# Gates, heads and output tiles in a fused attention-and-gate kernel: when the small work is done

## The chip, the cores and the metric

The kernel runs on one core of a Trainium2 chip. The time is the device time of one execution in microseconds (us); a kernel is judged by the median of its runs. The core has a matrix engine (TensorE, PE in the profile, with its weight loads as PEld), VectorE (DVE), ScalarE (ACT), GpSimd (POOL), SyncE (SP, which issues most transfers here), each with its own queue of instructions, and 16 queues of DMA. An engine works through its instructions in the order of the program; between engines semaphores say when a result is there.

## The reference

The input `x` has S = 2048 rows of D = 576 numbers. With `xn` its layer norm:

```python
qkv = (xn @ wqkv).reshape(1, S, 3, 32, 18)      # 32 heads of 18
p = softmax(q @ k.T * 18 ** -0.5)               # per head, 2048 x 2048
s = concat_heads(p @ v) @ wo
gate = relu(xn @ W_gate); up = xn @ W_up        # 576 -> 4608
g = silu((gate * up) @ W_down)                  # 4608 -> 576
out = x + s * g
```

All of it is float32.

## The kernel before

**Precision.** A float32 operand is kept as a high and a low part that TensorE can take, and a product is made of three matmuls (high x high, high x low, low x high). So every operand is *split* first: a rounding copy on one engine and a subtraction on another or the same. Weights are split on POOL (`split_pool`, lines 97 and 98).

**Stages.** Layer norm and the projections to q, k and v come first (to about 222 us of the span); their results go to DRAM (`qd`, `kd`, `vd`). Then the main loop, and at its end the output projection.

**Units.** The main loop has 144 units k = 0 to 143. A unit is one pair of a row group g (512 rows, in the order 3, 0, 1, 2) and one of 36 blocks f of 128 hidden features. It computes gate and up for them (`pg`, 54 matmuls in 27 pairs, the two halves of a pair on the upper and lower 64 rows of the array). Row groups therefore change at k = 36, 72 and 108. At the end of each even unit k > 0, `down(k - 1)` multiplies two blocks with W_down (`py`, 48 matmuls) and DVE adds the result to the four `y` tiles of the row group (line 501). When a row group is done, its four `y` tiles wait in the list `gates`; `gate_step` does one: tanh on ACT into the single buffer `e` (line 512), scale and product on POOL (513, 514), and a transfer of the gated tile to DRAM (`gd`, 515).

**Attention inside the units.** The 16 head pairs u are spread between these matmuls. From unit 16 on a head pair takes eight units (four for each half p of the rows), and a unit does, for each of two heads, 8 score matmuls `psx` with an exponential on ACT behind each (line 604) and 8 score matmuls `pm` of head pair u + 1 with a maximum on DVE behind each (line 194). A softmax needs the row maxima before the exponentials: `max_rows` turns them and stores them as two more rows of q. Units 0 to 15 have maxima of head pair 0 alone, 3 or 4 per head; units 136 to 143, the last head pair, have exponentials alone. Behind the 43 pairs of a unit (35 in the last head pair) come its 32 `po` matmuls, probabilities times v. Every fourth unit `finish` ends half a head pair: its second part `rest_`, and `max_rows`, are *tasks*, run at the end of the next even unit ahead of `down`.

**What sets the order.** `emit_unit` gives each score step a due slot among the unit's matmul pairs (the list `due`; a step with late = 0 is spread over all slots) and writes everything in that order; each engine follows the order of the program, and `i % 12 == 8` puts `gate_step` at slots 8, 20 and 32 (of 43). PSUM has 8 banks: five shared in turn by `pm`, `psx`, `py` and `pw` (`shared`), two for `pg` (`bank`, "gen"), and one for `po`, which takes one of the two `pg` of odd units below 16.

**Output.** `finish` splits the normalised heads and stores high and low part in `od` [2, 576, 2048]. After unit 143, 16 tiles of 128 rows are computed from `od` and `wo` (`pw`, 28 matmuls each), multiplied by the gated rows from `gd` (`gt`, line 746), added to `x` (747) and stored (748). Weights are loaded on SP in pieces of 128 columns, runs of 512 bytes.

Of the kernel before, what the change touches and what calls it, by code (L numbers as in the profile page):

```python
# [19 lines left out]
def kernel(  # L20
# [11 lines left out]
    P = 128  # L32
# [51 lines left out]
    od = dram.tile([2, D, S], F32, name="od")  # L84
# [113 lines left out]


    with ExitStack() as st:  # L200
# [169 lines left out]
        for g in range(NQ):  # L370
# [47 lines left out]
    def up_weights(k):
        if k >= len(units):
            return  # L420
        f = units[k][1]
        rg = wr.tile([P, KC, P], F32, name="rg")
        load2(rg, [[(wg, f * P, P)], [(wu, f * P, P)]])
        gw = ws.tile([P, 2, KC, P], F32R, name="gw")
        split_pool(gw[:, 0], gw[:, 1], rg)
        gus[k] = gw
# [15 lines left out]
    def up(k):  # L442
# [3 lines left out]
        ps = [bank("pg0"), bank("pg1") if k % 2 == 0 or k >= N1 else psO.tile([P, 512], F32, name="po")]  # L446
# [61 lines left out]
    def gate_step():  # L508
        if gates:
# [5 lines left out]
            nc.gpsimd.dma_start(gd[t * P : (t + 1) * P, :], y)  # L515

    vas = []
    for i in range(2):
# [4 lines left out]
        vas.append(va)  # L523
    def run_tasks():
# [4 lines left out]
    def max_rows(qT, mx):  # L529

        nm = two.tile([P, 2, 8], F32, name="nm")
        nx = two.tile([P, 2, 2, 8], F32, name="nx")
        vec(
            nc.vector.tensor_reduce(
                nm, mx.rearrange("p h b j c -> p h (b j) c"), axis=AX.X, op=ALU.max, negate=True
            )
        )
        nxr = nx.bitcast(F32R)
        vec(nc.vector.tensor_copy(nxr[:, :, 0], nm))
# [239 lines left out]
```

## Time and profile before

| | us |
|---|---|
| runs | 2700.24, 2700.65, 2705.1 |
| median | 2700.65 |
| profiled execution | 2709.15 |
| its span | 2707.4 |
| granted clock of TensorE over it | 0.992 |
| odd unit 35, even unit 36 | 13.94, 20.62 |
| unit 37 | 22.06 |
| end of the last `py` to the end of the span | 88.4 |

The profile is of one execution. Its span is what the traced instructions and transfers cover, the time has 1.75 us around it. In timelines a row begins with the start and the length in us, then engine, line, operation, what is written from what, its shape, and in brackets the idle time before it and whom it waited for. A unit's length is the distance between the first `pg` of it and of the next one. Groups give the busy time, the mean ns of one, and the idle time before them. Views of waits give the sum in us, how many, and the longest.

### The profile page before, as it was taken

The numbers are of one execution on the slowest core, as the hardware profiler recorded it, in microseconds if no ns is written. First come the engines' busy times: TensorE is split into PE (matmuls) and PEld (weight loads), VectorE is DVE, ScalarE is ACT, GpSimd is POOL, SyncE is SP. The second block draws the span as 40 slices with busy tenths as digits, with TensorE's granted clock in tenths as the row PEclk, the third lists the DMA queues.
The fourth block names the chain that finished last, engine by engine and source line by source line (L and its number), as shares of the span: only waits on it lengthen the run. The fifth ranks groups of instructions, "written<-read, shape, count | busy, mean of one in ns | idle before, by whom it ended". The sixth has DMA issues, their size and how long they took to land.

```text
span 2707.4 us, 54577 instructions
## 1 busy us (share of the span) xinstructions
PE 2646.0 (98%) x21852; PEld 2049.2 (76%) x21852; DVE 1947.7 (72%) x3218; ACT 1447.7 (53%) x2608; POOL 1308.3 (48%) x1084
## 2 busy tenths in 40 slices
PE   8999999999999999999999999999999999999996
PEld 6888887777767777777767777777776777777776
DVE  5426667888868888888877888888886888886211
ACT  3321125666656666666656666666656666666540
POOL 4235664444454444444454444444455444445643
PEclk9999999999999999999999999999999999999998
DMA  9745332323342222222262222222253232222247
GB/s 248 207 157 152 83 80 60 82 65 82 93 114 72 74 71 71 72 75 72 73 152 72 76 70 73 66 76 71 76 138 90 59 81 64 75 58 63 71 145 225
DMA packets 260094, 257.58 MB, mean 95 GB/s; under 512 B 30656, under 2 KB 201408, under 8 KB 259840
## 3 DMA queue, kind: packets, MB, share of 16 engines
q1 hardware_dynamic: 245632, 216.32, 31.0%
q0 software_dynamic: 14208, 37.78, 4.5%
q8 instruction: 172, 2.82, 0.5%
q14 instruction: 82, 0.67, 0.1%
HBM read 203.93 MB, written 49.55 MB: 94 GB/s over the span
## 4 chain that ended last, share of the span: by engine, by line
PE 89%; DMA 4%; POOL 3%; ACT 1%; issue 1%; SPq 1%; DVE 1%; POOLq 0%; DVEq 0%; ACTq 0%
PE pg L64 30%; PE po L64 18%; PE py L64 17%; PE pm L64 12%; PE psx L64 9%; PE pq L64 2%; PE pv L64 1%; DMA xr<-in_A_x_dram 1%; PE pw L64 1%; PE tps L70 1%; DMA rgw<-in_A_wqkv_dram 1%; DMA gt<-gd 0%; DMA rd<-in_B_W_down_dram 0%; DMA qd<-hh 0%; DMA qT<-qd 0%
## 5 line engine op out<-in xcount | busy, mean ns | idle before, releaser
L194 DVE TENSOR_REDUCE mx<-pm 128x1 f32<-128x512 f32 x2048 | 1368.4, 690 | 299.8 <-PE pg L64 133.2
L604 ACT ACTIVATE p<-psx 128x512 f32<-128x512 f32 x2048 | 1150.3, 599 | 496.8 <-PE psx L64 409.5
L64 PE MATMUL pg<-x,gw 64*128 64x512 f32 x7560 | 1389.4, 394 | 6.0 <-ACT r L470 3.7
L64 PEld LDWEIGHTS pg<-x,gw 64*128 64x128 f32 x7560 | 1080.4, 186 | 109.3 <-ACT r L470 7.2
L64 PEld LDWEIGHTS py<-dw,hh 128*128 128x128 f32 x3456 | 461.5, 188 | 63.9 <-issue 57.0
L64 PE MATMUL py<-dw,hh 128*128 128x288 f32 x3456 | 482.5, 298 | 2.7 <-DVE y L501 1.9
L97 POOL CAST gw<-rg 128x1152 fp32r<-128x1152 f32 x144 | 164.7, 1144 | 639.7 <-PE pg L64 539.7
L64 PE MATMUL po<-p,va 128*32 128x512 f32 x4096 | 471.5, 601 | 0.0
L64 PE MATMUL psx<-qT,kB 56*128 56x512 f32 x1120 | 442.7, 395 | 0.0
L64 PE MATMUL pm<-kB,qT 54*128 54x512 f32 x1120 | 429.0, 407 | 7.6 <-ACT p L604 7.6
L98 POOL TENSOR_TENSOR gw<-rg,gw 128x1152 fp32r<-128x1152 f32 x144 | 382.4, 2656 | 11.6
L64 PE MATMUL psx<-qT,kA 56*128 56x512 f32 x928 | 367.3, 396 | 0.0
L501 DVE TENSOR_TENSOR y<-py,y 128x288 f32<-128x288 f32 x544 | 233.2, 451 | 180.3 <-PE py L64 176.3
L64 PE MATMUL pm<-kA,qT 54*128 54x512 f32 x928 | 358.2, 409 | 4.8 <-ACT p L604 4.8
L64 PEld LDWEIGHTS po<-p,va 128*32 128x32 f32 x4096 | 120.7, 110 | 267.7 <-issue 259.9
L97 POOL CAST dw<-rd 128x576 fp32r<-128x576 f32 x144 | 95.9, 666 | 395.3 <-PE py L64 170.2
L64 PEld LDWEIGHTS pm<-kB,qT 54*128 54x128 f32 x1120 | 206.8, 185 | 63.8 <-issue 21.6
L64 PEld LDWEIGHTS psx<-qT,kB 56*128 56x128 f32 x1120 | 207.9, 186 | 12.8
L64 PEld LDWEIGHTS pm<-kA,qT 54*128 54x128 f32 x928 | 171.5, 186 | 54.6 <-issue 17.6
L98 POOL TENSOR_TENSOR dw<-rd,dw 128x576 fp32r<-128x576 f32 x144 | 206.0, 1430 | 11.7
L475 POOL TENSOR_TENSOR hh<-h,hh 128x512 fp32r<-128x512 f32 x144 | 185.5, 1288 | 9.1 <-ACT hh L474 9.1
L64 PEld LDWEIGHTS psx<-qT,kA 56*128 56x128 f32 x928 | 172.2, 186 | 12.2 <-ACT p L604 0.5
(86 smaller groups left out, 1602.6 us busy)
## 6 DMA issues: line engine op xcount, KB each, us to landing
rg<-in_B_W_gate_dram SPq DMA_DIRECT2D x144, 288.0 KB
rg<-in_B_W_up_dram SPq DMA_DIRECT2D x144, 288.0 KB
rd<-in_B_W_down_dram SPq DMA_DIRECT2D x144, 288.0 KB
x<-xTd SPq DMA_DIRECT2D x54, 256.0 KB
qT<-qd SPq DMA_DIRECT2D x192, 72.0 KB
od<-ol POOLq DMA_DIRECT2D x128, 72.0 KB, 2.6
qd<-hh POOLq DMA_DIRECT2D x16, 512.0 KB, 3.9
kd<-hh POOLq DMA_DIRECT2D x16, 512.0 KB, 5.0
```

What stands on the lines that cost most here:

```text
L64: return tc.keep_in_program_order(nc.tensor.matmul(*args, **kw))
L70: return tc.keep_in_program_order(nc.tensor.transpose(*args))
L97: nc.gpsimd.tensor_copy(hi, raw)
L98: nc.gpsimd.tensor_tensor(lo, raw, hi.bitcast(F32), ALU.subtract)
L194: vec(nc.vector.tensor_reduce(mx[:, h, b, j, c : c + 1], ps, axis=AX.X, op=ALU.max))
L475: nc.gpsimd.tensor_tensor(hh[:, 1], h, hh[:, 0].bitcast(F32), ALU.subtract)
L501: vec(nc.vector.tensor_tensor(ys[j][:, cs], ps, ys[j][:, cs], ALU.add))
L604: nc.scalar.activation(pts[kt][:, 2 * h + b, :], ps, AF.Exp, scale=SCALE)
```

## The change

- **Gates**: one `gate_step` in each unit (slot 8), not three; six `y` buffers, not five; the four gated tiles of the last row group stay in SBUF (`kept`) and are not sent to `gd`.
- **Heads**: stored as they are, in `od` [576, 2048], by four transfers on SP at the start of the next unit (`later`, `store`); the split comes after they are loaded again (`heads`, a copy on ACT and a subtraction on DVE).
- **Row maxima**: the 16 numbers of a row are turned once, unsplit; the split is made on POOL on the turned tile, and the 8 transfers follow, at the start of the next unit.
- **Banks**: in odd units below 16 `pg` takes the `po` bank and a shared one (`pg2`).
- **Exponentials**: `late` is -4, which makes their due slots denser and leaves the last four free.
- **Output**: tiles 0 to 3 are computed between units 142 and 143; the others in the order 4 to 7, 12 to 15, 8 to 11, with heads loaded per tile, two tiles ahead (`fetch`); `x` is added in one POOL operation per tile. The weights of `wo` lie in the former place of `kB` and of one q tile, in one tile `kq`, and in `w4`. `up_weights(0)` and `(1)` are written earlier.

```diff
-    od = dram.tile([2, D, S], F32, name="od")
+    od = dram.tile([D, S], F32, name="od")
...
                 kA = at.tile([P, NQ, 512], F32R, name="kA")
-                kB = at.tile([P, NRING - NQ, 512], F32R, name="kB")
-                for kT in (kA, kB):
-                    nc.gpsimd.memset(kT.bitcast(F32), 1.0)
-                ring[:] = [kA[:, 0], *(kB[:, i] for i in range(NRING - NQ)), *(kA[:, i] for i in range(1, NQ))]
-                qTs[:] = [at.tile([P, 2, 2, 512], F32R, name=f"qT{i}") for i in range(2)]
+                kq = at.tile([P, NRING, 512], F32R, name="kq")
+                nc.gpsimd.memset(kA.bitcast(F32), 1.0)
+                nc.gpsimd.memset(kq[:, : NRING - NQ].bitcast(F32), 1.0)
+                ring[:] = [kA[:, 0], *(kq[:, i] for i in range(NRING - NQ)), *(kA[:, i] for i in range(1, NQ))]
+                qTs[:] = [
+                    kq[:, NRING - NQ :].rearrange("p (a b) s -> p a b s", a=2),
+                    at.tile([P, 2, 2, 512], F32R, name="qT"),
+                ]
...
-    yp = pool(mid, "yp", 5, "right")
+    yp = pool(mid, "yp", 6, "right")
...
-        ps = [bank("pg0"), bank("pg1") if k % 2 == 0 or k >= N1 else psO.tile([P, 512], F32, name="po")]
+        if k % 2 and k < N1:
+            ps = [psO.tile([P, 512], F32, name="po"), shared("pg2")]
+        else:
+            ps = [bank("pg0"), bank("pg1")]
...
-    def gate_step():
+    def gate_step(spill_=True):
         if gates:
             y, t = gates.pop(0)
             e = wl.tile([P, D], F32, name="e", bufs=1)
             tc.keep_in_program_order(nc.scalar.activation(e, y, AF.Tanh, scale=0.5))
             nc.gpsimd.tensor_scalar(e, e, 0.5, 0.5, op0=ALU.mult, op1=ALU.add)
             nc.gpsimd.tensor_tensor(y, y, e, ALU.mult)
-            nc.gpsimd.dma_start(gd[t * P : (t + 1) * P, :], y)
+            if spill_:
+                nc.gpsimd.dma_start(gd[t * P : (t + 1) * P, :], y)
...
+    nms = []
+    for i in range(2):
+        nms.append(two.tile([P, 2, 16], F32, name=f"nm{i}", bufs=1))
+        nc.gpsimd.memset(nms[i], 0.0)
+    later = []
+
+    def run_later():
+        while later:
+            later.pop(0)()
+
     def run_tasks():
         while tasks:
             fn, args = tasks.pop(0)
...
 
     def max_rows(qT, mx):
 
-        nm = two.tile([P, 2, 8], F32, name="nm")
-        nx = two.tile([P, 2, 2, 8], F32, name="nx")
+        nm = nms[0]
+        nms.reverse()
         vec(
             nc.vector.tensor_reduce(
-                nm, mx.rearrange("p h b j c -> p h (b j) c"), axis=AX.X, op=ALU.max, negate=True
+                nm[:, 0].rearrange("p (h m) -> p h m", h=2), mx.rearrange("p h b j c -> p h (b j) c"),
+                axis=AX.X, op=ALU.max, negate=True,
             )
         )
-        nxr = nx.bitcast(F32R)
-        vec(nc.vector.tensor_copy(nxr[:, :, 0], nm))
-        vec(nc.vector.tensor_tensor(nxr[:, :, 1], nm, nx[:, :, 0], ALU.subtract))
         nt_ = two.tile([P, 32], F32, name="nt")
-        vec(nc.vector.transpose(nt_, nx.rearrange("p h a m -> p (h a m)")))
-        for h in range(2):
-            r = h * R + KA
-            dst = qT[r : r + 2].bitcast(F32).rearrange("a b (j q t) -> a (b j) q t", q=4, t=32)
-            for q in range(4):
-                nc.sync.dma_start(
-                    dst[:, :, q], nt_[q * 32 + h * 16 : q * 32 + h * 16 + 16, :]
-                )
+        vec(nc.vector.transpose(nt_, nm.rearrange("p a m -> p (a m)")))
+
+        def rows_():
+            nr = two.tile([P, 2, 32], F32R, name="nr")
+            split_pool(nr[:, 0], nr[:, 1], nt_)
+            for a in range(2):
+                dst = qT[KA + a :: R].bitcast(F32).rearrange("h b (j q t) -> h (b j) q t", q=4, t=32)
+                for q in range(4):
+                    nc.sync.dma_start(dst[:, :, q], nr[q * 32 : q * 32 + 16, a, :].bitcast(F32))
+
+        later.append(rows_)
 
     def block32(name):
         return two.tile([P, 512], F32, tag="ot", name=name)
+
+    def store(on, u, p):
+        for s_ in range(4):
+            h, b = divmod(s_, 2)
+            f0 = (2 * u + h) * DH
+            g = 2 * p + b
+            nc.sync.dma_start(od[f0 : f0 + DH, g * 512 : (g + 1) * 512], on[s_ * 32 : s_ * 32 + DH])
 
     def finish(po, u, p):
         ot = block32("ot")
...
             )
             on = block32("on")
             vec(nc.vector.transpose(on, tq))
-            ol = two.tile([P, 2, 512], F32R, name="ol", bufs=1)
-            nc.scalar.activation(ol[:, 0], on, AF.Copy)
-            nc.gpsimd.tensor_tensor(ol[:, 1], on, ol[:, 0].bitcast(F32), ALU.subtract)
-            for s_ in range(4):
-                h, b = divmod(s_, 2)
-                f0 = (2 * u + h) * DH
-                g = 2 * p + b
-                nc.gpsimd.dma_start(
-                    od[:, f0 : f0 + DH, g * 512 : (g + 1) * 512].rearrange("i p s -> p i s"),
-                    ol[s_ * 32 : s_ * 32 + DH].bitcast(F32),
-                )
+            later.append(lambda: store(on, u, p))
...
+        run_later()
...
-            for cnt, gen, off, late in ((nm, mx, 0.0, LATE), (ns, ex, 0.25, 0)):
+            for cnt, gen, off, late in ((nm, mx, 0.0, LATE), (ns, ex, 0.25, -4)):
...
-            if i % 12 == 8:
+            if i == 8:
...
+    kept = {}
+
+    def heads(k, hf, raw5, o5):
+
+        ks = slice(k * P, (k + 1) * P)
+        raw = block32("ro").rearrange("p (c s) -> p c s", s=P)
+        nc.sync.dma_start(raw, od[:C4, ks].rearrange("(c p) s -> p c s", p=P))
+        for i in range(2):
+            nc.sync.dma_start(raw5[i * DT : (i + 1) * DT], od[C4:D, ks])
+        nc.scalar.activation(hf[:, 0], raw, AF.Copy)
+        nc.vector.tensor_tensor(hf[:, 1], raw, hf[:, 0].bitcast(F32), ALU.subtract)
+        nc.scalar.activation(o5, raw5, AF.Copy)
+        nc.vector.tensor_tensor(o5[DT:P], raw5[DT:P], o5[DT:P].bitcast(F32), ALU.subtract)
+
+    def project(k, hf, o5, gt, xt, last=False):
+
+        for m in range(2):
+            cs = slice(m * HC, (m + 1) * HC)
+            ps = shared("pw")[:, :HC]
+            prs = []
+            for c in range(4):
+                w = wos[c]
+                prs += [(hf[:, 0, c], w[:, 0, cs]), (hf[:, 0, c], w[:, 1, cs]), (hf[:, 1, c], w[:, 0, cs])]
+            prs += [(o5, wos[4][:, i, cs]) for i in range(2)]
+            for i, (l, w) in enumerate(prs):
+                mm(ps, l, w, start=(i == 0), stop=(i == len(prs) - 1))
+            vec(nc.vector.tensor_tensor(gt[:, cs], ps, gt[:, cs], ALU.mult))
+            if last:
+                nc.vector.tensor_tensor(gt[:, cs], gt[:, cs], xt[:, cs], ALU.add)
+        if not last:
+            nc.gpsimd.tensor_tensor(gt, gt, xt, ALU.add)
+        nc.sync.dma_start(out2[k * P : (k + 1) * P, :], gt)
+
+    def rows_of(k, gt, xt):
+        if k not in kept:
+            nc.sync.dma_start(gt, gd[k * P : (k + 1) * P, :])
+        nc.sync.dma_start(xt, x2[k * P : (k + 1) * P, :])
...
+        if not more:
+            spare = [xtile(xA).rearrange("p i (c s) -> p i c s", s=P) for _ in range(2)]
+            sy = [yp.tile([P, D], F32, name="y") for _ in range(2)]
+            sx = vas[0].rearrange("p t d -> p (t d)")[:, :D]
+            sr = two.tile([P, NT, HW], F32, tag="raw", bufs=1, name="r5").rearrange("p t d -> p (t d)")
+            s5 = [two.tile([P, P], F32R, name=f"o5{i}", bufs=1) for i in range(2)]
...
+            if not more and i == PER - 2:
+                for j in range(4):
+                    heads(j, spare[j % 2], sr[:, j % 4 * P : (j % 4 + 1) * P], s5[j % 2])
+                    rows_of(j, sy[j % 2], sx)
+                    project(j, spare[j % 2], s5[j % 2], sy[j % 2], sx)
...
+    run_tasks()
+    run_later()
     down(len(units) - 1)
...
+    for y, t in gates:
+        kept[t] = y
+    order = [*range(4, 8), *range(12, 16), *range(8, 12)]
+    ready8 = {}
+
+    def fetch(n):
+        k = order[n]
+        hf = xtile(xA).rearrange("p i (c s) -> p i c s", s=P)
+        gt = kept[k] if k in kept else (ws if n % 2 else wr).tile(
+            [P, 2, KC, P] if n % 2 else [P, KC, P], F32, tag="gw" if n % 2 else "rg", name="gt"
+        )
+        if k not in kept:
+            gt = gt.rearrange("p a c s -> p (a c s)") if n % 2 else gt.rearrange("p c s -> p (c s)")
+            gt = gt[:, :D]
         xt = pp.tile([P, 4, 512], F32, tag="p", name="xr").rearrange("p a s -> p (a s)")[:, :D]
-        nc.sync.dma_start(xt, x2[k * P : (k + 1) * P, :])
-        return gt, xt
-
-    heads(order[0])
+        rows_of(k, gt, xt)
+        heads(k, hf, sr[:, k % 4 * P : (k % 4 + 1) * P], s5[k % 2])
+        ready8[n] = hf, s5[k % 2], gt, xt
...
+    fetch(0)
+    fetch(1)
     while gates:
-        gate_step()
+        gate_step(False)
+    for n, k in enumerate(order):
+        project(k, *ready8.pop(n), last=n == len(order) - 1)
+        if n + 2 < len(order):
+            fetch(n + 2)
```

ACT at the first change of row group, from the end of unit 36 to unit 38; `p<-psx` are exponentials, `e<-y` is the tanh of a gate. Before:

```order
L604 ACTIVATE p<-psx 128x512 x3
L512 ACTIVATE e<-y 128x576
L604 ACTIVATE p<-psx 128x512 x5
L512 ACTIVATE e<-y 128x576
L604 ACTIVATE p<-psx 128x512 x4
L512 ACTIVATE e<-y 128x576
L604 ACTIVATE p<-psx 128x512 x3
L470 ACTIVATE r<-pg_9967 128x512
```

and after the change:

```order
L623 ACTIVATE p<-psx 128x512 x4
L522 ACTIVATE e<-y 128x576
L623 ACTIVATE p<-psx 128x512 x12
L480 ACTIVATE r<-pg_9948 128x512
L484 ACTIVATE hh<-h 128x512
L623 ACTIVATE p<-psx 128x512 x4
L522 ACTIVATE e<-y 128x576
L623 ACTIVATE p<-psx 128x512 x12
```

The second and third tanh have moved out of unit 37, one unit further each, and all 16 exponentials of a unit stand ahead of the reading of its `pg` (`r`).

DVE at the end of an even unit with tasks, between `h` of the unit and the additions of `py`. Before:

```order
L472 TENSOR_TENSOR h<-pg_5877,r 128x512
L534 TENSOR_REDUCE nm<-mx 128x16
L539 CAST nx<-nm 128x2x8
L540 TENSOR_TENSOR nx<-nm,nx 128x2x8
L542 STREAM_TRANSPOSE nt<-nx 128x32
L560 STREAM_TRANSPOSE tq<-ot 128x512
```

and after the change:

```order
L482 TENSOR_TENSOR h<-pg_5878,r 128x512
L555 TENSOR_REDUCE nm_2958<-mx 128x16
L561 STREAM_TRANSPOSE nt<-nm_2958 128x32
L589 STREAM_TRANSPOSE tq<-ot 128x512
L592 RECIPROCAL rc<-tq 128x16
```

The cast and the subtraction are gone from this place; the rest stands as it stood.

ACT at units 140 and 141 after the change (before, no split of heads stands there):

```order
L623 ACTIVATE p<-psx 128x512 x16
L480 ACTIVATE r<-pg_33934 128x512
L484 ACTIVATE hh<-h 128x512
L705 ACTIVATE x<-ro 128x512
L707 ACTIVATE o_33180<-r_33179 128x128
L623 ACTIVATE p<-psx 128x512
L705 ACTIVATE x<-ro 128x512
L707 ACTIVATE o_33181<-r_33179 128x128
L623 ACTIVATE p<-psx 128x512 x15
```

The splits of the heads for tiles 0 and 1 (`x<-ro` for features 0 to 511, `o<-r` for the other 64) stand ahead of the first exponential of unit 141 and between it and the other 15.

More of the change, by code (lines that the diff above doesn't have):

```diff
@@ L197, in max_steps, with up_weights @@
                     yield
+    units = [(g, f) for g in (NQ - 1, *range(NQ - 1)) for f in range(NF)]
+    gus, dws, hhs = {}, {}, {}
+    N1 = NU
+    def up_weights(k):
+        if k >= len(units) or k in gus:
+            return
+        f = units[k][1]
+        rg = wr.tile([P, KC, P], F32, name="rg")
+        load2(rg, [[(wg, f * P, P)], [(wu, f * P, P)]])
+        gw = ws.tile([P, 2, KC, P], F32R, name="gw")
+        split_pool(gw[:, 0], gw[:, 1], rg)
+        gus[k] = gw
     with ExitStack() as st:
@@ L408 @@
     pp = pool(mid, "pp", 4, "right")
-    w3 = pool(mid, "w3", 1, "right")
+    w4 = pool(mid, "w4", 1, "right")
     wl = pool(mid, "wl", 2, "right")
-    yp = pool(mid, "yp", 5, "right")
-    units = [(g, f) for g in (NQ - 1, *range(NQ - 1)) for f in range(NF)]
-    gus, dws, hhs = {}, {}, {}
-    N1 = NU
+    yp = pool(mid, "yp", 6, "right")
     xcur = {NQ - 1: xs[NQ - 1]}
[L418 to L426, printed above, removed]
     def down_weights(k):
@@ L666, in out_weights @@
             nc.sync.dma_start(rd, wo[c * P : (c + 1) * P, :])
-            if c < 2:
-                w = kB.rearrange("p c s -> p (c s)")[:, c * 2 * D : (c + 1) * 2 * D]
-            elif c == 2:
-                w = qTs[0].rearrange("p a b s -> p (a b s)")[:, : 2 * D]
-            else:
-                w = w3.tile([P, 2 * D], F32R, name="wo3")
+            w = kq.rearrange("p c s -> p (c s)")[:, c * 2 * D : (c + 1) * 2 * D]
         else:
@@ L675, in out_weights @@
                 nc.sync.dma_start(rd[d * DT : (d + 1) * DT, :], wo[C4:D, :])
-            w = wr.tile([P, KC, P], F32R, tag="rg", name="wo4").rearrange("p c s -> p (c s)")
+            w = w4.tile([P, 2 * D], F32R, name="wo4")
         w = w.rearrange("p (i d) -> p i d", i=2)
@@ L689 @@
         k += 1
+    early4 = []
     for u in range(NU):
@@ L696 @@
                 out_weights(i)
-            if not more and i == PER - 1:
+            if not more and i == 4:
                 out_weights(4)
             emit_unit(k, ex, 64 // PER, mx, 64 // PER if more else 0)
+            if not more and i == PER - 2:
[3 more added lines that the diff above has]
+                    project(j, spare[j % 2], s5[j % 2], sy[j % 2], sx)
             k += 1
@@ L702 @@
             assert next(gen, None) is None
+    run_tasks()
+    run_later()
     down(len(units) - 1)
-    run_tasks()
-    order = (0, 1, 3, 2)
-    hfs, o5s = {}, {}
-    def heads(g):
-        gs = slice(g * 512, (g + 1) * 512)
-        hfs[g] = []
-        for c in range(4):
-            hf = xtile(xA)
-            nc.sync.dma_start(hf.bitcast(F32), od[:, c * P : (c + 1) * P, gs].rearrange("i p s -> p i s"))
-            hfs[g].append(hf)
-        o5s[g] = hp.tile([P, 512], F32R, tag="h", name="o5")
-        for i in range(2):
-            nc.sync.dma_start(o5s[g][i * DT : (i + 1) * DT].bitcast(F32), od[i, C4:D, gs])
```

28 lines of the change are left out of this document (3 added, 25 removed).

## The prediction

> **What bounds the kernel now.** I read the page first, then the span in stretches, one unit of the main loop each, then the waits and the timeline where a stretch was too long.
>
> ```profile
> PE 2646.0 (98%) x21852; PEld 2049.2 (76%) x21852; DVE 1947.7 (72%) x3218; ACT 1447.7 (53%) x2608; POOL 1308.3 (48%) x1084
> PE 89%; DMA 4%; POOL 3%; ACT 1%; issue 1%; SPq 1%; DVE 1%; POOLq 0%; DVEq 0%; ACTq 0%
> ```
>
> TensorE is busy 98% of the span and is 89% of the chain that ended last. The change leaves the number of its matmuls as it is, so it can win only the time in which PE waits or runs slowly, and that must be looked for stretch by stretch. Columns after the stretch: length, then busy time of PE, PEld, DVE, ACT and POOL, the granted clock, DMA share and GB/s.
>
> ```profile
> 726.76:740.70 13.94, 13.94 (x121) 9.73 (x120) 11.70 (x18) 10.18 (x18) 7.65 (x6) 1.00 0.80 190
> 740.70:761.32 20.62, 20.62 (x171) 15.88 (x167) 18.94 (x32) 11.42 (x20) 8.26 (x8) 1.00 0.75 168
> 761.32:783.38 22.06, 17.69 (x119) 10.14 (x118) 11.66 (x18) 11.35 (x21) 18.77 (x19) 0.85 0.53 143
> 783.38:804.08 20.70, 20.70 (x171) 16.43 (x167) 11.33 (x17) 13.41 (x26) 8.23 (x8) 1.00 0.32 83
> 1391.13:1412.54 21.41, 16.58 (x120) 10.02 (x120) 11.65 (x18) 11.35 (x21) 17.66 (x19) 0.84 0.55 148
> 2020.26:2039.72 19.46, 16.22 (x121) 9.56 (x120) 11.66 (x18) 11.30 (x21) 17.33 (x18) 0.91 0.47 134
> 2619.00:2699.30 80.30, 64.33 (x449) 63.03 (x447) 16.91 (x39) 3.25 (x5) 37.61 (x47) 0.94 0.77 236
> ```
>
> An ordinary odd unit (35) takes 13.94 us and an even one (36) 20.62, both with PE full. The odd units 37, 73 and 109, the first odd ones after a change of row group, take 22.06, 21.41 and 19.46. The output projection at the end has 64.33 us of PE in 80.30.
>
> **Gates.** In those three units three tanh stand among the 16 exponentials of the unit. From 400 to 2500 us (units 17 to 136) the list of PE's waits has one line, and the timeline of unit 37 shows one of its three times:
>
> ```profile
> PE pm L64 <- ACT p L604: 12.4, 3, 4.8
> 774.53 0.68 ACT L512 ACTIVATE e<-y 128x576 f32<-128x576 f32 x1 [4.41 <-POOL y L514]
> 772.35 0.66 POOL L513 TENSOR_SCALAR e<-e 128x576 f32<-128x576 f32 x1
> 773.10 1.40 POOL L514 TENSOR_TENSOR y<-y,e 128x576 f32<-128x576 f32 x1
> 737.12 3.64 PE L64 MATMUL po<-p,va 128*32 128x512 f32 x32
> 777.32 6.13 PE L64 MATMUL po<-p,va 128*32 128x512 f32 x32
> ```
>
> The third tanh wants the one buffer `e`, which POOL still multiplies for the second gate, behind a weight split. ACT idles 4.41 us with exponentials queued behind it, the score banks fill, PE waits, and afterwards the 32 attend matmuls take 6.13 us and not 3.64, at the granted clock of 0.85 above. Against 13.94 the three units lose 8.12 + 7.47 + 5.52 = 21.1 us. With one tanh per unit, `e` has a whole unit (13.9 us or more) to be freed, where POOL needs some 2.1 us (0.7 scale, 1.4 product), so the wait goes. What stays is the tanh's own time on ACT. Unit 38 has one tanh and no end-of-half tasks and takes 20.70; unit 36 has tasks and takes 20.62, of which the tasks are 0.16 (next part): one tanh costs about 0.24. Twelve of them now, three before: 9 more, 2.2 us. As the exponentials stand closer now (below), I allow 2.6. Net gain **18.5**; bounds 12 (tanh at its full 0.68 twelve times) and 21.
>
> Next late: `y`. The first block of the new group takes four `y` tiles at the end of unit 38, two of them free (six buffers); the other two need the spills of gates 0 and 1, issued in units 37 and 38, well over 10 us earlier. I cost that at nothing. Cover gone, ACT's copies of `py` would hold PE a few us at three places (rival 3).
>
> **Row maxima.** The cast and the subtraction on 16 numbers per row go from DVE; POOL does a small split, behind the weight split, and SP sends the same 8 small transfers a unit later. The rows are read four units or more later for one half and two for the other, so that is hidden.
>
> ```profile
> L539 DVE CAST nx<-nm 128x16 fp32r<-128x16 f32 x32 | 49.1, 1536 | 1.1
> L540 DVE TENSOR_TENSOR nx<-nm,nx 128x16 fp32r<-128x16 f32 x32 | 38.7, 1208 | 1.1
> 478.49 6.71 PE py L64 x48
> 513.10 6.55 PE py L64 x48
> 298.77 2.66 PE L64 MATMUL py<-dw,hh 128*128 128x288 f32 x18 [1.65 <-DVE y L501]
> PE pg L64 <- ACT r L470: 3.7, 8, 0.5
> ```
>
> DVE works at these (2.7 us a time) while `py` banks wait for its additions: a `py` block with tasks takes 6.71, one without 6.55. 31 of the 32 are such, 31 x 0.16 = **5.0** (bounds 0 and 5). The other is unit 6, where PE waits 1.65. The last row is the first phase: even units wait for both "gen" banks until ACT has read the odd unit's, 3.7 in all. Odd units now use two other banks. Together **5.4** (bounds 3 and 7, for what else the 0.5-us waits cost). `pg2` takes a shared bank from the maxima there, with 3 or 4 maxima per unit and half: nothing.
>
> **Heads unsplit.** ACT loses a copy, POOL a subtraction and four issues; SP gains four stores in front of its weight loads.
>
> ```profile
> L578 POOL DMA_DIRECT2D od<-ol x128 | 76.1, 597 | 10.5 <-POOL ol L573 9.3 <-issue 1.1
> 2690.43 0.46 SPq L724 DMA_DIRECT2D xr<-in_A_x_dram  x1
> ```
>
> POOL gives up 4 x 0.60 us of issues per half, but is 48% busy and stands on the path only at the gates, counted already. SP's later loads shift by 4 x 0.46 = 1.8 us every fourth unit, and are due a unit later. Nothing, on both sides; if a weight came 1.8 us late each time, 32 x 1.8 would be rival 1's size, but no such wait is listed now.
>
> **Exponentials due four slots earlier.** The odd unit's 13.94 less 3.64 of attends leave some 10.1 us for 43 pairs of matmuls, 0.234 a slot. Sixteen exponentials over 42 slots are one per 0.615 us, over 38 one per 0.557.
>
> ```profile
> 2570.70 8.11 ACT L604 ACTIVATE p<-psx 128x512 f32<-128x512 f32 x16 [5.14 <-PE psx L64]
> L604 ACT ACTIVATE p<-psx 128x512 f32<-128x512 f32 x2048 | 1150.3, 599 | 496.8 <-PE psx L64 409.5
> L194 DVE TENSOR_REDUCE mx<-pm 128x1 f32<-128x512 f32 x2048 | 1368.4, 690 | 299.8 <-PE pg L64 133.2 <-PE pm L64 96.1 <-PE psx L64 30.7
> ```
>
> ACT can do one per (8.11 - 0.60) / 15 = 0.50, so it still keeps up, with half the margin. The maxima share the five banks and DVE needs up to 0.69 for one, with one due per 0.72 when they are the denser kind. In the program's order a bank is asked for again 12 to 17 matmuls after its last writer, as before, on average 0.7 fewer. Between nothing and 0.3 us a unit (the margin of 0.06 lost for five banks) in some 120 units lies 0 to 36 us; since PE waits nowhere in these units now, I take 0.025 a unit, **-3**.
>
> **Tail.** Four of 16 tiles of the output projection go between units 142 and 143, the rest is fed tile by tile, split on ACT and DVE.
>
> ```profile
> 2612.36 6.64 PE L64 MATMUL py<-dw,hh 128*128 128x288 f32 x48
> 2612.53 0.60 ACT L556 ACTIVATE ot<-po 128x512 f32<-128x512 f32 x1 [1.26 <-PE po L64]
> 2619.42 0.70 DVE L560 STREAM_TRANSPOSE tq<-ot 128x512 f32<-128x512 f32 x1
> 2620.93 0.71 DVE L570 STREAM_TRANSPOSE on<-tq 128x512 f32<-128x512 f32 x1
> 2644.60 0.96 PE L64 MATMUL pw<-kB,x 128*128 128x288 f32 x6
> 2646.46 0.96 PE L64 MATMUL pw<-kB,x 128*128 128x288 f32 x6
> 2652.85 1.80 PE L64 MATMUL pw<-kB,x 128*128 128x288 f32 x6 [4.38 <-DVE gt L746]
> 2656.34 0.96 PE L64 MATMUL pw<-kB,x 128*128 128x288 f32 x6
> 2697.86 0.43 PE L64 MATMUL pw<-wo,o 128*128 128x288 f32 x2
> PE pw L64 <- DVE gt L746: 11.7, 3, 5.9
> PE pw L64 <- DMA o<-od: 3.2, 1, 3.2
> DVE gt L746 <- DMA gt<-gd: 54.1, 12, 14.2
> q1 hardware_dynamic: 10099, 20.08, 67.9%
> q1 hardware_dynamic: 9227, 7.39, 28.6%
> ```
>
> Half a tile is 2646.46 - 2644.60 = 1.86 us of PE, a tile 3.73, sixteen 59.7. From the end of `py` (2619.0) to the span's end (2707.4) are 88.4 now, of which PE waits 14.9, for `gt` above all, and loses about 5 more to the clock after waits; 9.1 lie behind the last matmul (2698.3). After: four tiles cost 14.9 before unit 143. Behind `py` PE then waits for the first heads. Their split on ACT stands in its order behind three tanh, and each tanh behind POOL's work for the one before (0.68 + 0.66 + 1.40 and gaps, 2.9 apart). The tasks now come before the additions of `py` on DVE: `ot` at 2613.1, 2.2 us of chain (2619.42 to 2621.64), first `y` done at about 2616.3, tanh at 2616.4, 2619.3 and 2622.2, the split from 2622.9 to 2623.6: a wait of **4.6** behind 2619.0. The heads themselves, stored from 2615.4 on, have till 2622.9 to come back. After a wait of that length PE is slow: the half tile behind the wait of 4.38 took 2656.34 - 2652.85 = 3.49, 1.6 more than 1.86. So 4.6 + 1.6, 12 x 3.73 = 44.8, further stalls of 2 (estimate, one of today's short ones), and 9.1: 62.1. Gain 88.4 - 14.9 - 62.1 = **11.4**. Stalls are fewer than today because `gt` is loaded ahead for four tiles and kept in SBUF for four. Bounds: heads at once and no stall, 19; today's waits of 14.9 and the 5 of slow clock again, 0.
>
> The trace has two prices for transfers: in the last 95 us 20.08 MB took 67.9% of 16 queues, 19.5 KB per us and queue; from 1000 to 1100 us, with mostly weights in runs of 512 bytes, 7.39 MB took 28.6%, 16.1. In the new tail's 4.6 + 44.8 + 3.6 = 53.0 us some ten tiles of heads in 512-byte runs (3.3 MB, 12.7 us on 16 queues) and 24 pieces of 288 KB (7.1 MB, 22.7 us) must move: 35.4 of 53.0 us or 67%, where today's share is 0.77. The Trainium skill, "DMA: Bandwidth & Descriptors", Rules for kernel authors, says to coalesce and that a transfer under 64 KB is mostly overhead, which speaks against the two 32-KB loads of heads per tile; its section on the anatomy of a DMA gives some 2 us fixed for each. By that the last 12 tiles' 24 small loads would add up to 48 us, an estimate, if each stood alone; no row here shows such loads one after another, and the sum does without it.
>
> **Against it:** the splits for the first two moved tiles stand in ACT's order ahead of, and just behind the first of, the exponentials of unit 141, and wait for heads stored at the end of unit 140 and loaded back. In that unit ACT is full (16 exponentials in one row of 8.11 us without a gap), so what it waits, PE waits soon after. The nearest row is today's wait for heads stored just before, 3.2; I take **-3**, bounds 0 and 5 (that wait and 1.6 of slow clock). Later the moved tiles' own chain (two `y`, one row buffer) lets their last two products wait some us, but unit 143 needs one bank at once: nothing, at most 5.
>
> **Sum:** 18.5 + 5.0 + 5.4 - 3 + 11.4 - 3 = 34.3. The profiled execution took 2709.15 (span 2707.4 and 1.75 around it), 8.5 above the median of 2700.65. Most terms are waits of fixed length, so I subtract from each: 2675 by the profile, **2666** by the median.
>
> **Rivals.**
> 1. Exponentials starve the banks. One mechanism: ACT's margin of 0.06 per exponential and DVE's of 0.03 per maximum do not carry the copies between them, and PE waits in every unit with scores. From 0.31 us in each of 120 units, 37 us with the 3 counted, the gain is gone; at 0.5 the time is 2666 + 57 = 2723. For it: the margin is halved. Against it: no PE wait in 2100 us but the three. Chance 0.07, the only way to slower that I see.
> 2. The tail runs at the transfers' pace: small runs twice as dear (25 us), with queues 77% busy, (25 + 23) / 0.77 = 62 us, 9 over the 53.0: 2675. For it: DVE waits 54.1 us on `gt` today at that share. Against it: today's waits are for buffers, too. Chance 0.17. (Of the Trainium skill's rules, the one above on small transfers would work this way.)
> 3. The gate change does not do what it says: a tanh is still late in each group, or the new `y` wait; from half of the 18.5 to all of it stays away: 2675 to 2685. Chance 0.08.
> 4. The moved tiles hold units 141 and 143 for 10 us in all, 7 more than counted: 2673. Chance 0.08.
>
> **How the numbers follow.** The forecast's case, 2654 to 2675 (half of each term's distance to its bounds), has 0.54; a larger gain (most terms at their better bound: 21 + 5 + 7 + 19 = 52, 2649) 0.07. Rivals 2 to 4 end at 2685 or below. The range 2649 to 2687 leaves out rival 1 and a little at both ends. About 0.2%, 5.4 us, is what a measurement of this kernel tells from no change: faster 0.91 (all but rival 1 and part of what is left), within 0.03, slower 0.06.
>
> **What would show it.** Right: units 37, 73, 109 near 14.2 us with the granted clock at 1.00 and no row of PE waiting for ACT there; every `py` block at 6.55; no wait on `r` before 400 us; some 62 us from the last `py` to the end. Wrong: rows of PE `pm` or `psx` waiting for ACT or DVE over the whole span (rival 1); PE `pw` waiting for DVE or ACT behind loads of heads (2); a PE wait over 5 us in unit 141 or 143 (4).

## The result, and the profile after

| | before | changed |
|---|---|---|
| median, us | 2702.88 | 2657.2 |
| lowest to highest, us | 2700.24 to 2710.15 | 2653.63 to 2657.88 |
| profiled execution, us (span) | 2709.15 (2707.4) | 2657.01 (2655.2) |

The ratio of the times is 0.9824, with a 95% interval of 0.9802 to 0.9847: 45.7 us faster by the medians, where 2666 was forecast, against the median of 2700.65 then known a gain of 34.3. The time lies in the range that was given, and the gain is larger than the sum. The profiled execution of before lay 6 us above its median, so the two profiles are 52.1 us apart.

The page of the changed kernel, its first line on busy time and the chain that ended last:

```profile
PE 2623.1 (99%) x21852; PEld 2023.3 (76%) x21852; DVE 1910.0 (72%) x3186; ACT 1399.6 (53%) x2608; POOL 1208.4 (46%) x971
PE 95%; DMA 2%; POOL 1%; DVE 1%; issue 0%; ACT 0%; SPq 0%; POOLq 0%; DVEq 0%; ACTq 0%
```

The number of matmuls is the same; PE's share of the chain has risen from 89% to 95%. The same stretches as before, of the changed kernel: units 35, 36, 37, 73 and 109, and the tail (columns as in the prediction):

```profile
721.93:735.76 13.83, 13.83 (x121) 9.63 (x120) 11.74 (x18) 9.85 (x18) 7.53 (x6) 1.00 0.75 174
735.76:756.19 20.43, 20.43 (x170) 15.88 (x167) 17.01 (x30) 10.44 (x19) 7.40 (x8) 1.00 0.82 183
756.19:770.25 14.06, 14.06 (x119) 9.57 (x119) 11.53 (x18) 10.17 (x19) 10.16 (x9) 1.00 0.65 168
1373.53:1387.60 14.07, 14.07 (x120) 9.26 (x119) 11.53 (x18) 10.17 (x19) 10.10 (x9) 1.00 0.63 162
1990.62:2004.70 14.08, 14.08 (x120) 9.29 (x120) 11.53 (x18) 10.17 (x19) 10.08 (x9) 1.00 0.39 110
2604.00:2651.00 47.00, 46.94 (x336) 46.45 (x334) 26.58 (x47) 9.93 (x22) 20.00 (x14) 0.95 0.68 210
```

The three units after a change of row group have lost their excess and have a clock of 1.00. An ordinary odd unit is 13.83 and not 13.94, an even one 20.43 and not 20.62, which nothing in the sum foresaw for the odd ones. All the waits of PE in the changed kernel:

```profile
PE tps L70 <- ACT xn L280: 12.7, 3, 11.3
PE pw L64 <- ACT x L705: 4.3, 1, 4.3
PE tps L70 <- ACT xn L283: 4.1, 1, 4.1
PE psx L64 <- DVE y L722: 2.2, 1, 2.2
PE pg L64 <- POOL gw L98: 2.0, 1, 2.0
PE pg L64 <- POOL gw L97: 1.3, 1, 1.3
PE psx L64 <- ACT p L623: 0.3, 1, 0.3
PE psx L64 <- DVE h L482: 0.2, 1, 0.2
```

The lines on `pm` behind exponentials (12.4), on `r` (3.7), on `py` and on `gt` (11.7) are gone. What is new is short: `pw` behind a split of heads on ACT, and `psx` of unit 143 behind the moved tiles.

Stretch by stretch, after minus before in the two profiles (unit starts read from the first `pg`): start to unit 0, 226.47 - 222.12 = +4.4; units 0 to 15, 165.5 - 172.2 = -6.7; units 16 to 135, 2058.6 - 2094.4 = -35.8; units 136 to 140, -1.9; from unit 141 to the end, 125.4 - 137.5 = -12.1. The sum is -52.1. The first of them is not counted as a gain or loss of the change: up to there the programs differ in little more than where things lie in memory and the weights of units 0 and 1, which the changed kernel asks for earlier, and unit 0 starts between 219.8 and 226.7 in the seven profiles with the old start and between 219.9 and 227.7 in the five with the new one.

### The profile page after: what moved, and what is told of

The parts are those of the page before. It is cut to its first block, busy times and chain, and to the rows that moved or that the text cites. A ratio compares the mean times of both kernels' runs of the same rounds, so it can differ in the third digit from the quotient of the medians.

```text
span 2655.2 us, 54665 instructions
## 1 busy us (share of the span) xinstructions
PE 2623.1 (99%) x21852; PEld 2023.3 (76%) x21852; DVE 1910.0 (72%) x3186; ACT 1399.6 (53%) x2608; POOL 1208.4 (46%) x971
## 4 chain that ended last, share of the span: by engine, by line
PE 95%; DMA 2%; POOL 1%; DVE 1%; issue 0%; ACT 0%; SPq 0%; POOLq 0%; DVEq 0%; ACTq 0%
PE pg L64 31%; PE po L64 18%; PE py L64 17%; PE pm L64 11%; PE psx L64 9%; PE pq L64 4%; PE pv L64 2%; PE pw L64 2%; PE tps L70 1%; DMA rd<-in_B_W_down_dram 0%; POOL dw L98 0%; DMA rgw<-in_A_wqkv_dram 0%; POOL gw L98 0%; DMA kd<-hh 0%; DMA rg<-in_B_W_up_dram 0%
## 5 line engine op out<-in xcount | busy, mean ns | idle before, releaser
L623 ACT ACTIVATE p<-psx 128x512 f32<-128x512 f32 x2048 | 1096.6, 603 | 583.9 <-PE psx L64 538.3
L64 PEld LDWEIGHTS pg<-x,gw 64*128 64x128 f32 x7560 | 1023.6, 187 | 108.1 <-issue 3.0
L98 POOL TENSOR_TENSOR gw<-rg,gw 128x1152 fp32r<-128x1152 f32 x144 | 382.6, 2657 | 11.7
L64 PE MATMUL psx<-qT,kq 56*128 56x512 f32 x608 | 231.1, 394 | 0.0
L64 PE MATMUL pm<-kq,qT 54*128 54x512 f32 x608 | 228.8, 399 | 0.1
L484 ACT ACTIVATE hh<-h 128x512 fp32r<-128x512 f32 x144 | 90.9, 631 | 220.5 <-DVE h L482 220.5
L64 PE MATMUL psx<-kq,kA 56*128 56x512 f32 x512 | 196.7, 395 | 0.3 <-DVE h L482 0.2
L64 PE MATMUL psx<-kq 56*128 56x512 f32 x512 | 195.5, 394 | 0.0
L64 PE MATMUL pm<-kq 54*128 54x512 f32 x512 | 194.6, 402 | 0.0
L64 PE MATMUL pm<-kA,kq 54*128 54x512 f32 x512 | 194.1, 400 | 0.0
L64 PE MATMUL psx<-qT,kA 56*128 56x512 f32 x416 | 160.1, 398 | 2.6 <-DVE y L722 2.2
```

The source lines that it names most:

```text
L64: return tc.keep_in_program_order(nc.tensor.matmul(*args, **kw))
L98: nc.gpsimd.tensor_tensor(lo, raw, hi.bitcast(F32), ALU.subtract)
L484: nc.scalar.activation(hh[:, 0], h, AF.Copy)
L623: nc.scalar.activation(pts[kt][:, 2 * h + b, :], ps, AF.Exp, scale=SCALE)
```

## The experiments

**Exponentials alone.** The kernel before with one number changed.

```diff
-            for cnt, gen, off, late in ((nm, mx, 0.0, LATE), (ns, ex, 0.25, 0)):
+            for cnt, gen, off, late in ((nm, mx, 0.0, LATE), (ns, ex, 0.25, -4)):
```

> The kernel before with the exponentials due four slots earlier, and nothing else. Profile of the changed kernel: an ordinary odd unit 13.84 us where before had 13.94, an even one 20.40 where before had 20.52 without tasks. Theory A (the packing does it, by a cheaper order of the matmuls): units 13.84 and 20.42, with tasks 20.58; some 120 units x 0.1 = 12 us faster, the group-change units still 19 to 22. Theory B (my prediction's sign: packing costs 0.025 a unit, and the 0.1 comes from another part): units 13.94 or a little more, the whole 0 to 4 us slower.

2691.73 us against 2700.93 (ratio 0.996, 0.9946 to 0.9974). Units 35, 36 (with tasks) and 37 of this kernel, its only long wait of PE in the main loop, and the end of the pairs of unit 45; the last fence has the same place in unit 45 of the kernel before:

```profile
725.95:739.81 13.86, 13.86 (x120) 9.99 (x120) 11.75 (x18) 9.86 (x18) 7.51 (x6) 1.00 0.80 195
739.81:760.49 20.68, 20.68 (x172) 15.94 (x168) 19.03 (x32) 11.08 (x20) 8.41 (x8) 1.00 0.70 167
760.49:779.39 18.90, 16.20 (x121) 9.35 (x120) 11.80 (x18) 11.07 (x21) 16.84 (x18) 0.91 0.54 165
PE pm L64 <- ACT p L604: 10.3, 3, 4.7
913.12 0.40 PE L64 MATMUL pm<-kB,qT 54*128 54x512 f32 x2
913.46 3.64 PE L64 MATMUL po<-p,va 128*32 128x512 f32 x32
```

```profile
917.68 0.52 PE L64 MATMUL pm<-kB,qT 54*128 54x512 f32 x2
918.13 1.07 PE L64 MATMUL po<-p,va 128*32 128x512 f32 x8
```

Theory A for the units' lengths: an odd unit takes 13.83 on average and an even one without tasks 20.43 (before 13.94 and 20.53), 0.1 less each, and the sign in the prediction's sum was wrong. An even unit with tasks stays at 20.68, so alone this is worth 0.1 in some 87 units, about 9 us, and not the 12 of all 120 (by the medians the whole kernel gains 9.2). The rest of the 13 us between the two profiles' units 16 to 135 is the three group-change units, 58.5 in all for 62.9. The place shows too: from the last two `pm` to the attends 913.46 - 913.12 = 0.34, where before had 0.45. With four free slots no score step of the exponentials stands among the last, and the two `pm` there get their banks sooner; that this is why is argued, not shown. With the row maxima moved as well, the units with tasks gain the 0.1 too: 20.49 in the rows-alone kernel, 20.39 in the kernel with four parts below.

**Gates alone.** The kernel before, five `y` buffers, without a third tanh in odd units.

```diff
-            if i % 12 == 8:
+            if i == 8 or (k % 2 and i == 32):
```

> The kernel before with at most two gates in an odd unit (slots 8 and 32) and one in an even one, so that no third tanh stands in units 37, 73 and 109; five y buffers stay. Theory A (the single e buffer and the third tanh make the stall): units 37, 73, 109 at 14.4 us or less with the granted clock at 1.00, no PE wait for exponentials, 18 to 20 us faster in the profile. Theory B (it is POOL's load or the y spills at the group change, and not the third tanh): a wait stays in units 37 to 39, less than 8 us won.

2687.6 us (ratio 0.9946, 0.993 to 0.9963). Unit 37, and the one line of PE's waits from 400 to 2500 us:

```profile
762.53:776.64 14.11, 14.11 (x121) 9.53 (x120) 11.73 (x18) 10.75 (x20) 12.77 (x15) 1.00 0.72 199
PE py L64 <- DVE y L501: 0.3, 1, 0.3
```

Theory A, to the size in the profiles: units 37, 73 and 109 take 14.10 to 14.11 and units 16 to 135 2074.2 for 2094.4. By the medians it is 13.3 us (2687.6 for 2700.93). Three tanh in one unit made the stall. The edit also puts 24 slots and not 12 between the two that stay, and lowers POOL's load in that unit (12.77 us for 18.77), so it doesn't tell these apart; for the single buffer `e` speaks the third tanh of unit 37 before, which waited 4.41 us for POOL's product of the second.

**Row maxima alone.** The kernel before with `max_rows`, `nms`, `later` and `run_later` of the changed one.

```diff
-        vec(nc.vector.tensor_copy(nxr[:, :, 0], nm))
-        vec(nc.vector.tensor_tensor(nxr[:, :, 1], nm, nx[:, :, 0], ALU.subtract))
...
+            split_pool(nr[:, 0], nr[:, 1], nt_)
...
+        later.append(rows_)
```

> The kernel before with the row maxima turned once, split on POOL and stored a unit later, and nothing else. Theory A (the cast and the subtraction on DVE hold up the additions of py): every py block with tasks 6.55 instead of 6.71, unit 6 at 14.4 instead of 16.3; 5.0 + 1.9 = 7 us faster. Theory B (the rest of the tasks on DVE is enough to hold py up): py stays at 6.65 or more, 2 us or less.

2690.77 us (ratio 0.9957, 0.9942 to 0.9972). A `py` block with tasks, unit 6, unit 37, and PE's wait for exponentials:

```profile
475.10 6.56 PE py L64 x48
283.67:298.00 14.33, 13.84 (x111) 12.19 (x108) 9.47 (x18) 2.46 (x4) 10.82 (x10) 1.00 0.28 82
757.18:775.40 18.22, 16.09 (x119) 9.70 (x118) 11.82 (x18) 11.18 (x21) 15.25 (x15) 0.91 0.53 160
PE pm L64 <- ACT p L615: 6.7, 3, 2.4
```

Theory A holds: `py` with tasks is 6.56 as without, unit 6 went from 16.30 to 14.33. That is 31 x 0.16 + 2 = 7. The other 3 are a second effect that neither theory had: the group-change units are 18.2 to 18.5 here, with waits of 6.7 and not 12.4. The three units take 55.0 in all here, 62.9 in the kernel before, 58.5 and 58.7 in the exponentials-alone and the banks-alone kernel, which leave the gates as they were: the stall is not the same in each execution, and how much of the difference is chance stays open. The profiled execution of before has the largest of them, and lay above its median: what is read from it for the gates is at the upper end.

**Banks alone.** The kernel before with the two banks for odd units below 16.

```diff
-        ps = [bank("pg0"), bank("pg1") if k % 2 == 0 or k >= N1 else psO.tile([P, 512], F32, name="po")]
+        if k % 2 and k < N1:
+            ps = [psO.tile([P, 512], F32, name="po"), shared("pg2")]
+        else:
+            ps = [bank("pg0"), bank("pg1")]
```

> The kernel before with the two other banks for pg in odd units below 16, and nothing else. Theory A (the 0.5-us waits on r are all there is): the even units of the first phase 14.56 and 14.38 become 13.9 to 14.1, 3.7 us faster. Theory B (the waits cost more than their length, by what stands behind them): 13.8 and 13.6 as in the changed kernel, some 5 to 6 us. Theory C (the shared bank pg2 delays the maxima): no gain.

2698.64 us (ratio 0.9992, 0.9981 to 1.0002): not told apart from before by the times. The profile tells more; units 4 and 6, and two waits of PE before 400 us:

```profile
263.54:277.37 13.83, 13.83 (x113) 12.42 (x110) 10.26 (x18) 2.46 (x4) 10.57 (x8) 1.00 0.33 87
284.36:299.84 15.48, 13.82 (x110) 12.51 (x107) 12.53 (x20) 2.47 (x4) 10.54 (x8) 1.00 0.29 78
PE pg L64 <- POOL gw L97: 3.5, 1, 3.5
PE pg L64 <- POOL gw L98: 1.5, 1, 1.5
```

Units 4 to 14 take 0.8 less each (14.62 to 13.83, 16.30 to 15.48), theory B; six of them are 4.8 us. But unit 1, which gains too, only waits longer for its weights: POOL's split ends when it ends, and unit 2 starts at 237.8 as before. Of a gain ahead of a wait for something else nothing arrives.

**Four parts, old tail.** The kernel before with these four (gates as in the gates-alone kernel).

> The kernel before with four parts together: exponentials due earlier, no third tanh in an odd unit, the row maxima on POOL a unit later, two other banks for pg below unit 16. Heads and output projection as before. Theory A (the parts add, each at its own place, and the rest of the gain is the tail's): unit 16 to 136 as in the changed kernel, 2058 to 2060 us where before had 2094; the end from unit 143 on 104 to 107 us as before; the whole 9 to 12 us slower than the changed kernel, 33 to 37 us faster than before. Theory B (heads stored unsplit take load from POOL and ACT and carry part of the gain inside the units): 2064 us or more between units 16 and 136.

2662.74 us (ratio 0.9846, 0.9828 to 0.9865). Units 16 to 135 take 2057.7, where the changed kernel has 2058.6: theory A. The parts inside the loop add up, by the times too (the four ratios multiply to 0.9856), and the unsplit heads carry nothing there. The tail is the old one:

```profile
PE pw L64 <- DVE gt L761: 8.7, 3, 6.4
PE pw L64 <- DMA o<-od: 4.8, 1, 4.8
```

From unit 141 to the end it takes 136.6, the changed kernel 125.4. So the new tail is worth 11.2 us by the profiles. By the medians it is 5.5 (2662.74 and 2657.2), less than the 9 to 12 expected, and the intervals of the two ratios overlap: the tail's gain is read from one execution each.

**The tail, three ways.** All three are the changed kernel with edits. The first computes no tiles between units 142 and 143:

```diff
-            if not more and i == PER - 2:
-                for j in range(4):
...
-    order = [*range(4, 8), *range(12, 16), *range(8, 12)]
+    order = [*range(0, 8), *range(12, 16), *range(8, 12)]
```

> The changed kernel with all 16 tiles of the output projection at the end, in the order 0 to 7, 12 to 15, 8 to 11, none between units 142 and 143. Theory A (moving only shifts matmul time and costs the two waits it makes): unit 141 at 11.9 instead of 13.0, unit 143's pairs at 8.4 instead of 12.9, 14.9 us more behind them, no new stalls: 5 us faster than the changed kernel. Theory B (the tail is paced by transfers, and 16 tiles in a row run into it): PE waits of more than 5 us behind loads of heads or of gated rows, no faster or slower.

the second moves the last gates behind the first tiles:

```diff
-    while gates:
-        gate_step(False)
     for n, k in enumerate(order):
...
         if n + 2 < len(order):
             fetch(n + 2)
+        gate_step(False)
```

> The changed kernel with the last four gates issued one each after the first four projected tiles, and not ahead of them. Theory A (the first pw waits for its split behind three tanh on ACT): the wait of 4.34 us falls to 1 to 2 us, the clock stays, 4 to 6 us faster. Theory B (the load of the heads stored just before sets that wait): the wait stays above 3.5 us, 0 to 1 us faster.

and the third does both.

> Both of the two: all 16 tiles at the end, and the last gates after the first tiles. Theory A (the waits are separate): 10 us faster than the changed kernel, PE from the end of the last py to the last matmul 59.7 us of matmuls and 1 to 2 of wait. Theory B (gates and loads then collide later in the tail): the gain of one is lost again, PE waits in the middle of the tail.

| from | changed | no tiles moved | gates later | both |
|---|---|---|---|---|
| median, us | 2657.2 | 2655.5 | 2652.98 | 2654.46 |
| unit 141 | 12.97 | 12.00 | 13.74 | 11.98 |
| unit 142 and moved tiles | 33.34 | 18.49 | 33.35 | 18.49 |
| unit 143 to the end of the span | 79.06 | 96.87 | 77.57 | 92.18 |
| sum | 125.4 | 127.4 | 124.7 | 122.7 |

The ratios to before are 0.9826 (0.9803 to 0.985), 0.9818 (0.9799 to 0.9837) and 0.9812 (0.979 to 0.9834): by the times none is told apart from the changed kernel. The profiles order them, one execution each. Waits of PE ahead of `pw`, without moved tiles, then with later gates:

```profile
PE pw L64 <- ACT x L705: 7.7, 4, 4.3
PE pw L64 <- DVE x L706: 0.8, 4, 0.2
PE pw L64 <- DVE o L708: 0.7, 1, 0.7
```

```profile
PE pw L64 <- DVE o L708: 1.6, 1, 1.6
PE pw L64 <- ACT x L705: 1.3, 1, 1.3
```

Without moved tiles the two waits that moving makes are gone, 5.4 us, but theory A fails: new waits of 4.9 us (9.2 listed, less the 4.3 ahead of the first tile) and slow clock behind them stand in the middle of the tail, and the sum is 2 worse. With later gates the wait ahead of the first tile falls from 4.3 to 1.3, theory A for the cause; but the clock behind it still falls to 0.50 for 3.4 us (2604.44 to 2607.85), a new wait of 1.6 takes half of the gain, and unit 141, which the edit doesn't touch, is 0.8 longer in this profile (`psx` waits 0.74 for an addition of `py`): 0.7 is left. Both together are 2.7 better, where theory A said 10.

**A tail with more room.** No moved tiles, heads loaded into the `xr` buffers (four and not two), one gate after every third tile.

```diff
-        raw = block32("ro").rearrange("p (c s) -> p c s", s=P)
+        raw = raw.rearrange("p (c s) -> p c s", s=P)
...
+        xt, raw = xp[:, :D], xp[:, D : D + 512]
...
+        if n % 3 == 1:
+            gate_step(False)
```

> The changed kernel with all 16 tiles at the end, heads loaded beside the rows of x (four buffers and not two), and the last four gates after the tiles 2, 5, 8 and 11 of the tail. Theory A (in the two kernels without moved tiles PE waits in the middle of the tail because two head buffers and the tanh in ACT's order hold the splits back): PE waits in the tail fall from 7 to 9 us to 3 or less, from unit 143 to the end 87 to 89 us, 6 to 8 us faster than the changed kernel. Theory B (the transfers themselves are the pace): the waits stay at 6 us or more, from unit 143 on 92 us or more.

2653.97 us (ratio 0.9813, 0.9795 to 0.9832), from unit 143 on 92.2: theory B by its number, but neither theory by the waits of PE, 4.2 ahead of `pw`. PE's waits from unit 143 on, ACT's for loaded heads and the whole tail of this kernel, then ACT's waits in the changed kernel's tail:

```profile
PE pw L64 <- ACT x L705: 2.8, 2, 1.4
PE pw L64 <- DVE x L706: 1.4, 4, 0.9
PE py L64 <- DVE y L511: 1.7, 1, 1.7
ACT x L705 <- DMA xr<-od: 41.4, 12, 5.1
2571.00:2639.00 68.00, 63.62 (x452) 61.54 (x450) 30.86 (x64) 13.84 (x31) 30.28 (x23) 0.97 0.68 206
```

```profile
ACT x L705 <- DMA ro<-od: 19.3, 8, 4.2
ACT o L707 <- DMA r<-od: 6.5, 2, 5.0
```

With buffers to spare ACT still waits for heads to land, but little of it reaches PE: from the last `py` to the last matmul it takes 67.4 us for 59.7 of matmuls, 4.2 of the rest in waits and some 1.7 (an estimate) at a clock of 0.50 that lasts 3.4 us; the other 1.8 are not listed anywhere. The 1.7 ahead of that is another matter: a split of heads on DVE stands between the additions of `py`. The transfers' pace is not shown: queues are at 0.68 over this tail as in the changed kernel's 47 us, which has 5 us at 0.97 (2615 to 2620) without a wait. The two tiles of heads that PE waited for, 1.4 us each, were asked for late: SP issues their loads at 2606.98 and 2611.97, behind the store of a finished tile, and their splits begin 4.2 and 5.1 us later. How much of that is the order on SP and how much the transfers stays open. So does the worth of moving four tiles: in the profiles it gains 2.0 with the gates first (125.4 for 127.4) and loses 2.0 with the gates late (124.7 for 122.7).

**The end of the span.** In the kernel before, 9.1 us lie between the last matmul and the end, in the changed one 4.3. The trace shows POOL's closing drain until 2706.58, 9.2 us behind POOL's last addition (2697.34); in the changed kernel 3.3 (2649.23 to 2652.51), within the landing of the last output. The kernel before with the transfers of gated tiles and heads issued by SP:

```diff
-            nc.gpsimd.dma_start(gd[t * P : (t + 1) * P, :], y)
+            nc.sync.dma_start(gd[t * P : (t + 1) * P, :], y)
...
-                nc.gpsimd.dma_start(
+                nc.sync.dma_start(
                     od[:, f0 : f0 + DH, g * 512 : (g + 1) * 512].rearrange("i p s -> p i s"),
```

> The kernel before with the transfers of gated tiles and of heads issued by SP and not by POOL, to see what the end of the span hangs on: before, 9.1 us lie between the last matmul and the end, with POOL's closing drain 9.2 us behind its last addition; the changed kernel has 4.3. Theory A (POOL's late software transfers lengthen its drain): 4 to 5 us behind the last matmul. Theory B (something else, such as POOL's many additions): 7.7 us or more as in all four kernels with the old tail.

2688.34 us, one run. The drain ends 2.3 us behind POOL's last addition (2680.47 to 2682.77). The span ends 6.0 us behind the last matmul, between the two theories, but 3.0 behind DVE's last addition (2683.53, late by a row of `x`), as in the changed kernel (3.3), and not 8.1 as before: theory A for the drain, on this single execution. Unit 37, and PE's waits for exponentials in the whole run:

```profile
758.50:776.22 17.72, 16.19 (x120) 9.62 (x119) 11.71 (x18) 11.19 (x21) 14.56 (x13) 0.90 0.64 177
PE pm L64 <- ACT p L604: 4.6, 3, 1.9
```

The three group-change units take 51.5 in all, less than in any other kernel that keeps the gates (55.0 to 62.9). POOL's issues no longer stand between its products there; that this is why is argued, since the stall differs between executions.

## Why the prediction was right, point by point

- **Gates**, 18.5 forecast. The stall of 21.1 went, and one tanh in each of twelve units costs 0.23 (units 37 to 40 take 69.4 for 68.5 without), where before had three such units outside the stall (0.5): 21.1 + 0.5 - 2.8 = 18.8. The mechanism is right, shown by the gates-alone kernel; the size is right for the profiled execution. I subtracted the stall from the median as a wait of fixed length, and it is not one: by the medians the gates-alone kernel gains 13.3.
- **Row maxima**, 5.0, and unit 6: right, shown by the rows-alone kernel.
- **Banks and first phase**, 5.4 in all with unit 6. Units 0 to 15 gained 6.7, since an even unit lost 0.8 and not 0.5 at `r`; it lay within the bounds (3 to 7).
- **Exponentials**, -3. This step failed. I priced the denser slots as a risk to the banks and gave it no chance to gain, though the bounds of an unknown cost should reach below nothing. It is +0.1 us a unit, shown by the exponentials-alone kernel for some 87 units (9 us) and, with the row maxima moved, for the units with tasks as well: 12 us, so 15 of the sum's error. What in the order makes the 0.1 is not shown. Rival 1 (starved banks) is refuted by the same rows. (The 10.1 us for the 43 pairs are 10.3 by the rows, 13.94 - 3.64; the step fails with either.)
- **Tail**, 11.4, with -3 for unit 141 and nothing for 143. Together 8.4; measured 12.1. The wait ahead of the first tile was 4.34 (forecast 4.6), behind three tanh on ACT as worked out; the slow clock behind it 2.7 (1.6); further stalls 0 (2). Unit 141 lost 1.0 (3), unit 143 4.4 (nothing, at most 5), of which 2.2 are a wait and some 1.7 (an estimate) the clock of 0.50 in the 3.4 us behind it. And 4.8 came from the end of the span, of which the sum had nothing: I took 9.1 behind the last matmul as fixed. That the losses of unit 143 and the gain at the end of the span nearly cancel is luck. Rival 4 (10 us in units 141 and 143) did not come: 5.4.

The two places, of the changed kernel: ACT and PE at the first tile, then DVE and PE in unit 143.

```profile
2602.23 0.68 ACT L522 ACTIVATE e<-y 128x576 f32<-128x576 f32 x1 [2.27 <-POOL y L524]
2602.82 0.61 ACT L705 ACTIVATE x<-ro 128x512 fp32r<-128x512 f32 x1
2603.49 3.55 PE L64 MATMUL pw<-kq,x 128*128 128x288 f32 x12 [4.34 <-ACT x L705]
2580.03 0.82 DVE L722 TENSOR_TENSOR y<-pw,y 128x288 f32<-128x288 f32 x2 [3.78 <-DMA y<-gd]
2580.54 0.86 PE L64 MATMUL psx<-qT,kA 56*128 56x512 f32 x2 [2.24 <-DVE y L722]
```

The split stands right behind the third tanh, which waited for POOL's product of the one before. In unit 143 `psx` wants a bank that a moved tile's product holds until its gated row is back from DRAM, through one of two `y` buffers.

- **Rival 2** (the tail at the transfers' pace) did not happen in the changed kernel, with queues at 0.68 over its 47 us and 0.64 over the 51.8 from the last `py` to the last matmul, where 67% were worked out for 53. With all 16 tiles at the end it is not shown either. On the Trainium skill's rule on small transfers ("DMA: Bandwidth & Descriptors", Rules for kernel authors): 24 small loads did not add their fixed times one after another; ACT waited 6.5 us in all for the 32-KB pieces, and PE not at all. (The 2 us fixed for each, by which the prediction makes 48 us, are given in the Trainium skill, "DMA: Bandwidth & Descriptors", Anatomy of one DMA, for transfers issued by GpSimd. These are issued by SP.)
- The base of 2700.65 was fair, and the range wide enough for a step of the wrong sign: further runs of before lay between 2695 and 2712. In the profiles the gain is 17.8 above the sum: 15 from the exponentials, 3.7 from the tail, 1.9 from units 136 to 140, 1.3 from units 0 to 15, 0.3 from the gates, less 4.4 from the stretch ahead of unit 0. (The chances of the cases add up to 1.01.)

## What to carry to other kernels

Where an engine is busy 98%, the gain is in the few stretches where it is not, and one tanh too many in another engine's queue can be such a stretch: look for a single buffer whose reader sits on a third engine. When work is moved in an in-order program, list what stands ahead of it on each engine it crosses; the wait of 4.3 us behind three tanh could be read off in advance. A cost that the trace doesn't show can also be a gain, and the bounds have to say so.

## What was not expected of the hardware

Software transfers issued by POOL lengthen the end of the program: its closing drain took 9.2 us behind its last operation in each of the six kernels where POOL sends the last heads and four gated tiles (53 to 70 us earlier in the kernel before), and 2.3 in the one where SP sends them; what the drain waits for so long after is not shown. And the same matmuls in another order cost 0.1 us less a unit, where the list of waits has no line for these units before or after: such a loss shows in the distance of rows, not in that list. A wait of 2.2 us (unit 143), and two of 1.4 within 6 us of each other (the tail with more room), were followed within 2 us by a granted clock of 0.50 for 3.4 us.
